# Attention, a wide MLP and a top-1 expert layer on one core: where the last rows are written, what GpSimd computes, and where the smallest expert runs

## The chip, the cores and the metric

The kernel runs on one core of a Trainium2 chip. The metric is the device time of one execution in microseconds (us). The kernel before took 583.51 us (median of three runs, 580.92 to 584.21); lower is better.

## The reference

```python
def _attn_ref(q, k, v, w1, b1, w2):                  # 2 x 8 heads, 576 positions, head size 64
    scores = (1.0 / np.sqrt(D)) * np.matmul(q, k.transpose(0, 1, 3, 2))
    x = (np.log1p(np.abs(rel)) / np.log1p(np.maximum(pos[:, None], 1.0)))[..., None]
    scores = scores + (np.maximum(x @ w1 + b1, 0.0) @ w2).transpose(2, 0, 1)[None]
    attn = softmax(scores)                           # over the keys
    return np.matmul(attn, v)

def _moe_ref(x, w_in, w_out):                        # 1152 x 512 -> 2048 -> 512
    h = x @ w_in
    sp = np.where(h > 20.0, h, np.log1p(np.exp(np.minimum(h, 20.0))))
    return (h * np.tanh(sp)) @ w_out

def _moe2_ref(x, w_gate, w1, w2, capacity):          # 8 experts, 512 -> 1024 -> 512, capacity 288
    expert_idx = np.argmax(x @ w_gate, axis=1)       # one expert per row
    # the first 288 rows of each expert are kept, the others give zero
    h = np.maximum(np.einsum('ecd,edf->ecf', disp, w1), 0.0)
    y = np.einsum('ecf,efd->ecd', h, w2)
    out[i] = gate_w[i] * y[expert_idx[i], pos[i]]    # gate_w: softmax probability of the expert

reference: x = attention heads joined to 1152 rows of 512; _moe_ref; _moe2_ref
```

## The kernel before

**Tiles.** Attention and the MLP go over five tiles of rows (`it` 0 to 4): four of 256 rows (128 of each batch) and one of 128, which holds the last 64 rows of both batches. Products that need precision are made of two half-precision terms: a "high half" (the value rounded to f16) and a "low half" (the rest), and three f16 matmuls high x high, high x low, low x high.

**Order.** Everything up to the first expert's inputs is a list of operations, each with one or more ways to run it (an engine, a cost in ns that the planner of the table believes, and the code). The table `ORDER` at the top holds, for every operation, its place and its way: `c // 8` is the operation, `c % 8` the way. `Plan.emit` issues them in that order, so each engine's queue is what the table says. Behind it (from line 1351) the experts are written in plain program order.

**MLP chain.** For each of 8 pairs of feature blocks (`mlp_a`, line 825) the chain from the first product's PSUM is: exp (ScalarE, 839), two steps on VectorE (840, 841), ln and exp (842, 843), a product (844, GpSimd or VectorE), a scaled product (845, VectorE), the high half (848) and the low half (849, GpSimd or VectorE), and then the second product (`mlp_b`). `split16` (316) makes the halves of the attention's output, `keys_split` (593) those of the keys, `slots` (1085) adds up which row goes to which place of the first expert (1100); all three have ways on GpSimd.

**Handover to the first expert.** `y_out` writes each tile's result rows to `yscr` in DRAM (951; for the last tile 981 and 982). The first expert is the one that row 0 chose. `first_rows` computes from the first four tiles which rows it gets (`gid0`, line 1136) and gathers them in three indirect DMAs from GpSimd (1139). `first_slots` then places them: for each of four blocks of 128 features it multiplies the three gathered chunks (f32, 96 rows each) with a masked unit matrix `dg` and the last tile's rows, still in SBUF (`yx`), with a 0/1 matrix `m_`, both in f32, into one PSUM bank; a high and a low half of that bank go to `xT`. `first_loads` has meanwhile loaded the expert's weights and made the halves of the first one (1246 to 1262).

**Experts.** `experts_list` (1327) sorts the chosen experts, the first first and the smallest last; its numbers go to registers. `expert(k)` loads the next first weight (`load1`), runs `gemm1(k)` (8 blocks of 12 matmuls; in it the halves of this expert's second weight, `halves(k, 1, i)`, and behind block 0 the last piece of the expert before, `finish(k - 1)`), reads the next token table, gathers the next rows (`gather`), loads the next second weight (`load2`) and runs `gemm2(k)` (4 groups of 24 matmuls; in it the next expert's halves, its transposed rows `xt`, and `back`, which transposes results to rows). `sized` computes a weight's scale from four sums of squares (`square`). `scatter` writes the rows to the output, three indirect DMAs. Token tables and lists (`tb`, `gid`, `tid`) have two buffers. If the last expert has at most 48 rows, `few` (1477) runs it: with the rows as the stationary operand, in f16 halves like the others. In these inputs four experts are chosen; three run in full and the fourth has few rows.

Of the kernel before, what the change touches and what calls it, by code (L numbers as in the profile page):

```python
# [9 lines left out]
F32 = mybir.dt.float32  # L10
# [12 lines left out]
P = 128  # L23
# [266 lines left out]
def tile_kernel(ctx: ExitStack, tc: tile.TileContext, a: dict, cap: int):  # L290
# [794 lines left out]
    def slots(t):  # L1085
# [3 lines left out]
        def f():  # L1089
            ts(dve, si.t[:, 1:2], si.t[:, 0:1].bitcast(U32), e0s, ALU.subtract)  # L1090
            if t == 8:
                ts(dve, m_.t[:, 0:SL], sl16, si.t[:, 1:2], ALU.is_equal)
                return
# [48 lines left out]
    def first_slots(m_):  # L1142
# [13 lines left out]
        for ct in range(4):  # L1156
# [8 lines left out]
            def f(ps=ps, cc=cc):  # L1165
                pe.matmul(ps.t[:, 0:SL], y_.t[:, cc], m_.t[:, 0:SL], start=False, stop=True)
# [452 lines left out]
```

## Time and profile before

| | |
|---|---|
| median of three runs | 583.51 us |
| profiled execution | 582.39 us |
| its span, first to last instruction | 580.6 us |
| TensorE busy (matmuls; weight loads) | 500.1 us; 339.8 us |
| VectorE, ScalarE, GpSimd busy | 457.9, 392.8, 114.3 us |
| TensorE clock granted, mean | 0.943 of 2.4 GHz |
| DMA | 74.27 MB, mean 128 GB/s |

PE is TensorE's matmuls, PEld its weight loads, DVE is VectorE, ACT ScalarE, POOL GpSimd, SP SyncE (which issues DMAs). An engine with a q behind it (POOLq, SPq) is its queue. A row of a timeline is one instruction, or several alike in a row (x24): start, length, engine, line, operation, output<-inputs, shapes, and in brackets how long the engine stood idle before and what ended that.

### The profile page before, as it was taken

To read this page: it belongs to the slowest core of one execution; us is meant where nothing else is said; L and a number is where in the kernel's file an instruction comes from. 1 tells how busy PE (TensorE), PEld (TensorE's weight loads), DVE (VectorE), ACT (ScalarE), POOL (GpSimd) and SP (SyncE) were. 2 spreads that over 40 slices of the span, in tenths; PEclk is the share of its full clock that TensorE was granted. 3 is DMA by queue.
4 is the path that set the end of the run, shared out by engine and by line. 5 is a ranking of instruction groups with operands and counts; after the bars stand their busy time and mean duration, and the time that the engine had idled before them with its cause. 6 is when DMAs were issued, how large, how long until landed. Compare 5 with 4: busy or idle time off the path is not lost. (4 is left out here: it accounts for less than half of the span.)

```text
span 580.6 us, 12111 instructions
## 1 busy us (share of the span) xinstructions
PE 500.1 (86%) x4521; PEld 339.8 (59%) x4521; DVE 457.9 (79%) x1163; ACT 392.8 (68%) x791; POOL 114.3 (20%) x143
## 2 busy tenths in 40 slices
PE   5565888989999988999999899999983598999775
PEld 4111556765666653555687557896472477777532
DVE  8999999998884898999869845699788275867363
ACT  5889999988575768999956714656741057877361
POOL 2000000011122326200011602125341201112120
PEclk9975699989999999999999999999997599999879
DMA  8987973700110123546244022050010147666210
GB/s 330 362 330 243 330 277 112 278 22 1 59 37 1 65 103 102 172 160 208 78 124 120 0 76 61 34 201 1 1 39 10 51 161 244 192 193 204 88 33 16
DMA packets 28347, 74.27 MB, mean 128 GB/s; under 512 B 4870, under 2 KB 4998, under 8 KB 26224
## 3 DMA queue, kind: packets, MB, share of 16 engines
q1 hardware_dynamic: 26576, 69.21, 34.8%
q0 software_dynamic: 1696, 4.11, 2.3%
q8 instruction: 40, 0.66, 0.5%
q14 instruction: 35, 0.29, 0.2%
HBM read 55.67 MB, written 17.87 MB: 127 GB/s over the span
## 5 line engine op out<-in xcount | busy, mean ns | idle before, releaser
L834 PEld LDWEIGHTS <-WIt 128*128 128x128 f16 x960 | 85.3, 98 | 15.2 <-issue 5.6
L867 PE MATMUL pb<-WOt,ra 128*128 128x512 f16 x336 | 78.0, 379 | 1.6 <-DVE ra L849 0.7
L834 PE MATMUL pb<-PX,WIt 128*128 128x256 f16 (+1 forms) x696 | 74.8, 265 | 3.0 <-DVE rr L306 1.7
L654 ACT ACTIVATE ra<-ra,rm 128x576 f32<-128x576 f32 x62 | 47.9, 774 | 17.8 <-DVE rm L653 17.8
L867 PEld LDWEIGHTS <-ra 128*128 128x128 f16 x336 | 31.9, 98 | 39.7 <-issue 3.7
L309 DVE SCALAR_TENSOR_TENSOR W<-AT,wsc,W 128x1024 f16<-128x1024 f32 x32 | 40.6, 1280 | 15.2 <-ACT W L1402 14.8
L517 PE MATMUL pb<-ra,w2s 128*32 128x512 f32 (+17 forms) x268 | 35.8, 541 | 16.0 <-ACT ra L506 6.9
L506 ACT ACTIVATE ra<-AT,stab 128x528 f32<-128x528 f32 (+16 forms) x67 | 41.2, 650 | 4.6 <-DVE PX L309 2.1
L653 DVE CUSTOM_DVE_ANT_0 ra<-ps,ra 128x576 f32<-128x576 f32 x50 | 36.5, 752 | 9.2 <-PE ps L636 8.2
L726 PE MATMUL pb<-ra,AT 128*64 128x128 f32 (+1 forms) x700 | 40.7, 267 | 0.7 <-ACT ra L665 0.7
L844 POOL TENSOR_TENSOR ra<-ra,ra 128x512 f32<-128x512 f32 (+1 forms) x13 | 15.5, 1195 | 129.1 <-DVE gl L323 90.3
L1446 PE MATMUL py<-HH,W 128*128 128x288 f16 x288 | 39.3, 294 | 0.9 <-ACT HH L1420 0.7
L726 PEld LDWEIGHTS pb<-ra,AT 128*64 128x64 f32 x700 | 35.2, 139 | 5.5 <-issue 1.8
L662 PE MATMUL pb<-ident,ra 128*128 128x128 f32 x201 | 31.8, 290 | 3.8 <-ACT ra L665 1.9
L1446 PEld LDWEIGHTS <-W 128*128 128x128 f16 x288 | 29.0, 101 | 8.9 <-issue 1.3
L1417 PEld LDWEIGHTS <-W 128*128 128x128 f16 x288 | 28.2, 98 | 9.5 <-DVE W L309 1.4
L1197 ACT ACTIVATE jk<-AT 128x1024 bf16<-128x1024 f32 x28 | 29.5, 1055 | 2.1 <-DMA AT<-m 1.9
L662 PEld LDWEIGHTS pb<-ident,ra 128*128 128x128 f32 x201 | 23.5, 147 | 11.4 <-ACT ra L654 4.8
L309 DVE SCALAR_TENSOR_TENSOR rw<-rw 128x1024 int32<-128x1024 int32 x24 | 29.2, 1222 | 0.3
L531 ACT ACTIVATE rbe<-pb,rl 128x511 f32<-128x511 f32 (+41 forms) x53 | 24.8, 489 | 6.0 <-PE pb L517 2.9
L834 PE MATMUL ps<-PX,WIt 128*128 128x256 f16 (+1 forms) x264 | 27.6, 258 | 0.0
L842 ACT ACTIVATE ra<-ra,two 128x512 f32<-128x512 f32 (+1 forms) x21 | 13.6, 646 | 17.9 <-DVE ra L309 14.8
(444 smaller groups left out, 1149.8 us busy)
## 6 DMA issues: line engine op xcount, KB each, us to landing
AT<-m SPq DMA_DIRECT2D x32, 512.0 KB, 4.7
bscr<-rbe SPq DMA_DIRECT2D x36, 295.5 KB, 2.2
rw<-wo SPq DMA_DIRECT2D x8, 1024.0 KB, 4.6
ra<-bscr SPq DMA_DIRECT2D x27, 288.0 KB, 3.4
rw<-wi SPq DMA_DIRECT2D x4, 1024.0 KB, 12.0
WOt<-wi SPq DMA_DIRECT2D x4, 1024.0 KB
AT<-k SPq DMA_DIRECT2D x4, 576.0 KB, 7.1
out<-rw SPq DMA_DIRECT2D x9, 256.0 KB, 3.2
```

What stands on the lines that cost most here:

```text
L309: (eng or dve).scalar_tensor_tensor(out=out, in0=in0, scalar=s, in1=in1, op0=op0, op1=op1)
L506: on_act = lambda h_=h_, g=g: act.activation(h_.t[:, 0:dn], T[:, 0:dn], AF.Relu, bias=stab[:, g:g + 1])
L517: pe.matmul(ps.t[32 * c:32 * c + 32, 0:d1 - d0], w2s, hs[c].t[:, d0:d1], start=True, stop=True)
L653: op("DVE", c_dve(S), lambda i=i, own=own, m_=m_, b_=b_: dve.tensor_tensor_reduce(out=own(), in0=blk(s_.t[:, 960 * i:960 * i + S]), in1=bl ...
L654: op("ACT", c_act(S, 2), lambda i=i, m_=m_, col=col: act.activation(t_.t[:, S * i:S * i + S], t_.t[:, S * i:S * i + S], AF.Exp, bias=m_.t[ ...
L662: pe.transpose(pa.t[:, P * j:P * j + P], t_.t[:, 384 * n + P * j:384 * n + P * j + P], ident)
L726: pe.matmul(ov[64 * i:64 * i + 64, ct % 2, w * bb:w * bb + w], v_, t_.t[:, at + c0:at + c0 + w], start=n == 0, stop=n == 4)
L834: pe.matmul(ps.t[:, n * f_:n * f_ + n], WI[:, wv, ct, P * ft:P * ft + P], xt.t[:, xv, ct, 0:n], start=i == 0, stop=i == 11)
L867: pe.matmul(y_.t, gv()[:, g2, c:c + P], WO[:, wv, ft], **kw)
L1197: act.activation(j.rearrange("p (a b) -> p a b", a=2) if m else j, raw(m, i), AF.Square, accum_out=sca(k, m, i))
L1417: pe.matmul(ps[:, 0:SL], W1[:, wv, ct, P * ft:P * ft + P], XT[k % 2][:, xv, ct], start=i == 0, stop=i == 11)
L1446: pe.matmul(ps[:, 0:SL], W2[:, wv, ft, P * dt:P * dt + P], HH[:, hv, ft], start=ft == 0 and i == 0, stop=ft == 7 and i == 2)
```

## The change

- The last tile's two writes to `yscr` wait until the three gathers of the first expert are through (`r=[y_] + [("g0", c) ...]`).
- The gathered rows and the last tile's rows are split into f16 halves first; `first_slots` places high and low halves with separate f16 matmuls (two groups per feature block), and their PSUM banks are copied to `xT` each by itself.
- The ways on GpSimd go from `split16`, `keys_split`, `mlp_a` (844, 849) and `slots` (1100). Some believed costs change. There is a new `ORDER` table.
- In the experts: token tables and lists have three buffers; for k above 0, `sized` moves from block 1 to block 2 of `gemm1` and the halves one block on; the second weight's third high half goes from ScalarE to VectorE; expert 1's four squares move from `gemm1(0)` to the start of `gemm2(0)`, its sizing one group on.
- `few` goes. The expert with few rows runs inside its neighbour (`with_few`): its weights are loaded to buffers of their own before the neighbour's first product, its rows are gathered behind that product, and its f32 matmuls stand between the groups of the neighbour's second product.

The table, decoded by operation, changes these engines: line 844 from 25 on GpSimd and 15 on VectorE to 40 on VectorE; line 849 from 28 and 12 to 40; line 1100 from 2 and 4 to 6; `split16` in `x_out` from 11 on GpSimd, 12 on VectorE, 1 on ScalarE to 15 on VectorE, 9 on ScalarE; line 602 from 8 on GpSimd to 3 on VectorE, 5 on ScalarE; line 531 from 21 on VectorE to 10, line 665 from 34 to 26, line 710 from 9 to 4, the others of these to ScalarE; line 1261 from 2 on VectorE to none. On VectorE, behind the last tile's routing, the new table has, in this order: one low half of the first weight, the row list, the last rows' high half, the low half of gather 0, `dg`, the halves of gathers 1 and 2, the last rows' low half, `m_`, the sizing of the second weight, the last low half of the first weight, three copies to `xT`.

```diff
-        op("POOL", c_pool(m, 2.1), lambda: pool.tensor_tensor(out=nv(), in0=nv(), in1=uv(), op=ALU.mult), r=[u_], w=[n_], alt=[("DVE", ...)])
+        op("DVE", c_dve(m), lambda: dve.tensor_tensor(out=nv(), in0=nv(), in1=uv(), op=ALU.mult), r=[u_], w=[n_], lk=1)
...
-            dma(lambda: yscr[512:576], lambda: yv()[:64], 131072, r=[y_], p=["yscr"])
+            h_ = pl.buf(R2)
+            hv = lambda v: h_.t.bitcast(F16)[:, DM * v:DM * v + DM]
+            op("ACT", c_act(DM, 1, 50), lambda: act.activation(hv(0), ps.t, AF.Identity, scale=col(1)), r=[ps, y_], w=[h_], alt=[("DVE", ...)])
+            op("DVE", c_dve(DM, 1.04, 1), lambda: stt(hv(1), ps.t, col(1), hv(0), ALU.mult, ALU.subtract), r=[ps, y_], w=[h_])
+            dma(lambda: yscr[512:576], lambda: yv()[:64], 131072, r=[y_] + [("g0", c) for c in range(NCH)], p=["yscr"])
...
+            for v in range(2):
+                ps = pl.buf(RB)
+                def f(ps=ps, cc=cc, v=v):
+                    for c in range(NCH):
+                        pe.matmul(ps.t[:, CS * c:CS * c + CS], xg0[c][1](v)[:, cc], dg.t.bitcast(F16)[:CS, CS * c:CS * c + CS], start=c == 0, stop=False)
...
+                    pe.matmul(ps.t[:, 0:SL], yv(v)[:, cc], m_.t.bitcast(F16)[:, 0:SL], start=False, stop=True)
...
-    tb = [es(f"tb{i}", [CS, NCH, 2], I32) for i in range(2)]
+    tb = [es(f"tb{i}", [CS, NCH, 2], I32) for i in range(3)]
...
-            if k and ft == 1:
+            if k and ft == 2:
                 sized(k, 1, PO[0])
...
-            if ft > 1 and ft < 6:
-                halves(k, 1, ft - 2)
-            if more and ft > 3:
+            if ft > 1 + bool(k) and ft < 6 + bool(k):
+                halves(k, 1, ft - 2 - bool(k))
+            if k and more and ft > 3:
                 square(k + 1, 0, ft - 4, W["j"])
...
+    def few_rows():
...
+        dve.tensor_copy(tidf, sel[:, 0, 0:1])
+        ts(dve, gidf, sel[:, 0, 0:1], float(NT - 1), ALU.min)
+        pool.indirect_dma_start(out=xgf, out_offset=None, in_=yscr, in_offset=bass.IndirectOffsetOnAxis(ap=gidf[:, 0:1], axis=0))
+    def few_x():
+        for ct in range(4):
+            pe.transpose(PT[0][:, CS * ct:CS * ct + CS], xgf[:, P * ct:P * ct + P], ident[:CS, :CS])
+        act.copy(XF.rearrange("p c n -> p (c n)"), PT[0][:, 0:4 * CS])
+    def few_h(i):
+        for ct in range(4):
+            pe.matmul(PH[i][:CS], XF[:, ct], R1f[:, ct, 512 * i:512 * i + 512], start=ct == 0, stop=ct == 3)
...
+    def few_y(i):
+        for ft in range(4 * i, 4 * i + 4):
+            pe.matmul(PH[0][:CS], HF[:, ft], R2f[:, ft], start=ft == 0, stop=ft == 7)
+    def with_few(k):
+        few_loads()
+        if k:
+            gemm1(k, False)
+        few_rows()
+        def between(dt):
+            if dt == 0:
+                few_x()
+            if dt < 2:
+                few_h(dt)
+            if dt:
+                (few_flip if dt < 3 else few_y)((dt - 1) % 2)
+        gemm2(k, False, between)
+        finish(k)
+        few_y(1)
+        act.activation(OC[:, 0], PH[0][:CS], AF.Copy, scale=sel[:, 0, 1:2])
+        pool.indirect_dma_start(out=a["out"], out_offset=bass.IndirectOffsetOnAxis(ap=tidf[:, 0:1], axis=0), in_=OC[:, 0], in_offset=None, ...)
...
-        with tc.If(nv > k + 1) as more:
+        with tc.If(nf > k + 1) as more:
...
-            if k:
-                last(k)
-            else:
-                gemm2_last(k)
+            with tc.If(nv > k + 1) as more_:
+                with_few(k)
+            with more_.Else():
+                last(k)
```

## Rows read from the trace of the kernel before

**Rows 1.** Stage windows: busy us of each engine (x instructions), granted clock, DMA share, GB/s.
```profile
200.00:280.00 80.00, 75.22 (x659) 41.14 (x658) 74.62 (x210) 68.31 (x152) 20.66 (x18) 1.00 0.44 148
280.00:440.00 160.00, 153.50 (x1668) 114.35 (x1667) 122.16 (x354) 91.15 (x195) 48.05 (x51) 1.00 0.21 63
...
444.50:455.40 10.90, 0.03 (x1) 0.00 (x0) 6.96 (x16) 0.00 (x0) 4.99 (x4) 0.50 0.23 67
455.40:464.80 9.40, 8.40 (x32) 7.21 (x33) 2.19 (x7) 1.12 (x3) 0.00 (x0) 0.61 0.08 16
...
559.00:574.20 15.20, 14.67 (x56) 7.51 (x56) 8.80 (x19) 5.21 (x9) 2.67 (x2) 0.80 0.14 38
```

**Rows 2.** Timelines of VectorE, SyncE, GpSimd and TensorE at the handover.
```profile
440.26 0.17 DVE L306 TENSOR_SCALAR gid<-smsk 96x3 uint32<-96x3 f32 x1
...
445.35 10.59 SPq L330 DMA_DIRECT2D yscr<-rw  x2
...
449.85 2.13 POOL L1139 DMA_INDIRECT ra<-yscr,gid  x1 [0.30 <-issue]
452.28 0.91 POOL L1139 DMA_INDIRECT ra<-yscr,gid  x1 [0.30 <-issue]
...
455.47 1.14 PE L1162 MATMUL pb<-rw,ra 96*128 96x96 f32 x4 [10.95 <-DMA ra<-yscr,gid]
...
464.86 3.10 PE L1417 MATMUL ph<-xT,W 128*128 128x288 f16 x24 [0.99 <-DVE xT L1169]
```

**Rows 3.** Timelines of TensorE, GpSimd and VectorE, third expert's second product.
```profile
533.92 3.10 PE L1446 MATMUL py<-HH,W 128*128 128x288 f16 x24
...
541.18 4.78 PE L1446 MATMUL py<-HH,W 128*128 128x288 f16 x24
...
536.60 0.94 POOL L1385 DMA_INDIRECT xg<-yscr,gid  x1 [0.79 <-issue]
...
540.58 0.17 DVE L1388 CAST tid<-tb 96x3 uint32<-96x3 int32 x1 [4.76 <-DMA out<-OC,tid]
```

**Rows 4.** Timeline of GpSimd: the last scatters.
```profile
560.90 1.74 POOL L1431 DMA_INDIRECT out<-OC,tid  x1 [2.07 <-DMA out<-OC,tid]
564.77 0.92 POOL L1431 DMA_INDIRECT out<-OC,tid  x1 [2.13 <-DMA out<-OC,tid]
575.11 0.92 POOL L1518 DMA_INDIRECT out<-OC,tid  x1 [9.42 <-ACT OC L1517]
```

**Rows 5.** Groups of instructions, whole span: xcount | busy us, mean ns | idle before.
```profile
L849 POOL TENSOR_TENSOR ra<-ra,ra 128x512 f16<-128x512 f32 x14 | 17.1, 1221 | 33.7 <-ACT ra L848 15.2 <-DVE ra L848 9.8 <-PE pb L968 5.4
...
L844 DVE TENSOR_TENSOR ra<-ra,ra 128x512 f32<-128x512 f32 x3 | 2.0, 675 | 0.0
...
L306 DVE TENSOR_SCALAR ra<-ra 128x512 f32<-128x512 f32 x14 | 8.4, 604 | 8.5 <-ACT ra L839 8.5
L306 DVE TENSOR_SCALAR ra<-rw 128x512 f32<-128x512 f32 x9 | 3.8, 423 | 5.4 <-ACT rw L839 5.4
...
L1166 PE MATMUL pb<-rw,rw 128*128 128x288 f32 x8 | 4.1, 634 | 0.0
...
L1169 DVE TENSOR_TENSOR xT<-pb,xT 128x288 f16<-128x288 f32 x4 | 1.7, 455 | 1.0 <-ACT xT L1168 1.0
```

**Rows 6.** Timeline of VectorE: end of the handover list, and of the third expert's first product.
```profile
446.39 0.75 DVE L306 TENSOR_SCALAR W<-AT,wsc 128x1024 f16<-128x1024 f32 x1
...
451.62 0.15 DVE L1325 COPY cnt<-pb 1x8 f32<-1x8 f32 x1
...
533.72 1.28 DVE L309 SCALAR_TENSOR_TENSOR W<-AT,wsc,W 128x1024 f16<-128x1024 f32 x1
534.92 0.82 DVE L309 SCALAR_TENSOR_TENSOR HH<-pt,HH 128x288 f16<-128x288 f32 x2
```

**Rows 7.** Timelines of TensorE (second product of the first expert) and VectorE (a sizing).
```profile
480.11 0.28 PE L1446 MATMUL py<-HH,W 128*128 128x288 f16 x1 [0.73 <-ACT HH L1420]
...
525.63 0.91 DVE L306 TENSOR_SCALAR wsc<-wsc 128x1 int32<-128x1 int32 x5
```

More of the change, by code (lines that the diff above doesn't have):

```diff
@@ L1099, in slots @@
         if t > 1:
[L1100 removed]
+            op("DVE", c_dve(SL, 0.52), lambda: dve.tensor_tensor(out=acc[b], in0=acc[b], in1=m_.t.bitcast(F16)[:, 0:SL], op=ALU.add), r=[m_], w=[("acc", b)], lk=1)
     xg0 = []
@@ L1347, in experts_list @@
         tsum(fl[:, 0:E], v64)
+        ts(dve, A, ef[0:1], 1.0, ALU.add, fl[:, E:E + 1], ALU.is_equal)
+        dve.tensor_tensor(out=A, in0=A, in1=fl[:, 0:E], op=ALU.mult)
+        tsum(fl[:, E + 2:E + 3], A)
+        ts(dve, fl[:, E + 1:E + 2], fl[:, E + 1:E + 2], float(HC + 1), ALU.is_lt)
+        dve.tensor_tensor(out=fl[:, E + 1:E + 2], in0=fl[:, E:E + 1], in1=fl[:, E + 1:E + 2], op=ALU.subtract)
         dve.tensor_copy(lst[:, 1:], fl[:, 1:])
@@ L1387, in tokens @@
     def tokens(k):
[L1388 removed]
+        dve.tensor_copy(tid[k % 3], tb[k % 3][:, :, 0])
     def summed(k, m):
@@ L1436, in back, with gemm2 @@
             pe.transpose(po[:, c], YT[:, dt, CS * c:CS * c + CS], ident)
-        dve.tensor_tensor(out=OC[:, :, P * dt:P * dt + P], in0=po, in1=tb[k % 2][:, :, 1:2].bitcast(F32).to_broadcast([CS, NCH, P]), op=ALU.mult)
-    def gemm2(k):
-        summed(k + 1, 0)
+        dve.tensor_tensor(out=OC[:, :, P * dt:P * dt + P], in0=po, in1=tb[k % 3][:, :, 1:2].bitcast(F32).to_broadcast([CS, NCH, P]), op=ALU.mult)
+    def gemm2(k, more=True, between=None):
+        if more:
+            if k == 0:
+                for i in range(4):
+                    square(1, 0, i, W["j"])
+            summed(k + 1, 0)
         for dt in range(4):
@@ L1447, in gemm2 @@
             act.activation(YT[:, dt], ps[:, 0:SL], AF.Copy, scale=sca(k, 0, 7))
-            if dt == 0:
-                sized(k + 1, 0, PO[1])
-            if dt == 2:
-                for c in range(NCH):
-                    xt(k + 1, c, (PT + PH)[c % 4])
-            if dt == 1 or dt == 2:
-                halves(k + 1, 0, 2 * dt - 2)
-                halves(k + 1, 0, 2 * dt - 1)
-            if dt > 1:
+            if more:
+                if dt == (k == 0):
+                    sized(k + 1, 0, PO[1])
+                if dt == 2:
+                    for c in range(NCH):
+                        xt(k + 1, c, (PT + PH)[c % 4])
+                if dt == 1 or dt == 2:
+                    halves(k + 1, 0, 2 * dt - 2)
+                    halves(k + 1, 0, 2 * dt - 1)
+            if dt > 0:
+                back(k, dt - 1)
+            if more and dt > 1:
                 square(k + 1, 1, 2 * dt - 4, W["j"])
                 square(k + 1, 1, 2 * dt - 3, W["j"])
-            if dt > 0:
-                back(k, dt - 1)
+            if between:
+                between(dt)
     def finish(k):
@@ L1511, in few, with few_loads @@
+    def few_loads():
+        sp.dma_start(tbf, tv[bass.ds(evf[0], 1)].rearrange("o p c w -> (o p) c w"))
+        for ct in range(4):
+            sp.dma_start(R1f[:, ct], a["m1"][bass.ds(evf[0], 1), P * ct:P * ct + P].rearrange("o p f -> (o p) f"))
+        for i in range(4):
+            sp.dma_start(R2f[:, 2 * i:2 * i + 2], a["m2"][bass.ds(evf[0], 1), 2 * P * i:2 * P * i + 2 * P].rearrange("o (c p) n -> p (o c) n", p=P))
+    def few_rows():
         for c, m in ((0, 0), (NCH - 1, 1)):
-            ts(dve, sel[:, c, 0:1], t_[:, c, 0:1], hm[:, m:m + 1], ALU.mult)
@@ new lines, in few_h, with few_flip @@
+    def few_h(i):
+        for ct in range(4):
+            pe.matmul(PH[i][:CS], XF[:, ct], R1f[:, ct, 512 * i:512 * i + 512], start=ct == 0, stop=ct == 3)
+        if i:
+            ts(dve, hs[:, 512:1024], PH[1][:CS], 0.0, ALU.max)
+        else:
+            act.activation(hs[:, 0:512], PH[0][:CS], AF.Relu)
+    def few_flip(i):
+        for j in range(4):
+            pe.transpose(PT[i][:, CS * j:CS * j + CS], hs[:, 512 * i + P * j:512 * i + P * j + P], ident[:CS, :CS])
+        dst, src = HF[:, 4 * i:4 * i + 4].rearrange("p f n -> p (f n)"), PT[i][:, 0:4 * CS]
+        if i:
+            dve.tensor_copy(dst, src)
+        else:
+            act.copy(dst, src)
@@ L1520, in last @@
     def last(k):
-        with tc.If(nl < HC + 1) as small:
-            few(k)
-        with small.Else():
+        if k:
             gemm1(k, False)
-            gemm2_last(k)
+        gemm2_last(k)
     def expert(k):
```

114 lines of the change are left out of this document (40 added, 74 removed), and 217 rows, old and new, of the table ORDER.

## The prediction

> **What bounds the kernel now.** I read the stage windows first, then the timelines of single engines where a stage has idle TensorE time, then the grouped instructions for prices. In the windows the reader sees three regimes [rows 1]. From 280 to 440 us TensorE is busy 153.5 of 160 us while VectorE has 122.2: the attention and MLP tiles are bound by TensorE, with little left to win. At the handover to the experts, 444.5 to 464.8 us, TensorE does 8.4 us of work in 20 us and its clock is granted at 0.50 to 0.61 (1.2 GHz for most of it). In the last expert, 559 to 574.2 us, the clock is 0.80 with TensorE nearly always busy.
>
> The timelines name the causes. At the handover the row numbers of the first expert (gid) are ready at 440.4 us, but the first of the two writes of the last rows, issued at 445.35 us, stands ahead of the gathers; the last two start at 449.85 and 452.28 us, and TensorE waits 10.95 us for them, until 455.47. The first expert starts at 464.86 [rows 2]. In the expert part TensorE has a hole at 537 to 540.8 us: VectorE's copy of the next token list waits 4.76 us for the scatter still reading its buffer; after the hole 24 matmuls take 4.78 us instead of 3.10 [rows 3]. At the end, scatters to the output go one after another, each waiting some 2.1 us for the one before [rows 4].
>
> The sum is made against the profiled execution, 582.39 us, with 580.6 of span and 1.8 around it; it lies 1.1 us under the median of 583.51 and inside the three runs.
>
> **GpSimd's arithmetic goes to VectorE (attention and MLP).** The issue table puts 53 products and differences of the MLP, 25 of line 844 and 28 of line 849, on VectorE, beside two sums of line 1100 and a few copies. On GpSimd one 128x512 takes 1.22 us, on VectorE 0.68 where it is least disturbed [rows 5]: at most 53 x 0.68 = 36 us more for VectorE. Against that the table moves 24 PSUM copies (11 of line 531, 8 of 665, 5 of 710) from VectorE to ScalarE, at about 0.5 us each (0.46 for 288 elements [rows 5]), 12 us. VectorE also gets back time that it now loses beside GpSimd: one form, 128x512 f32 of line 306, takes 604 ns in one group and 423 in another [rows 5], 2.5 us over 14 instructions in this group alone, and others are stretched alike. So VectorE's load grows by 24 us at most and perhaps not at all, against 38 us of idle time in 280 to 440 us [rows 1]. TensorE sets the pace there, with 6.5 idle us in that stretch and 4.8 in 200 to 280. The two GpSimd steps of each MLP chain become shorter by half, so part of these gaps should close, while the new order may open others. Bounds: 9 faster (nearly all gaps close), 6 slower (half as many again open). I take -3, near the small end, because what is gained in latency is mostly hidden behind TensorE.
>
> **Handover.** The write now follows the gathers, so these start some 0.8 us after gid (GpSimd's delay in the next such gather [rows 3]), at 441.2, with one every 1.24 us; the last lands 3.2 us after its start, as now (452.28 to 455.47) [rows 2], at 446.9. This wait is gone; next late is VectorE. It finishes its present list of small steps at 451.77 [rows 6]. The new list leaves out one high half and one low half of the first weight (0.74, 1.28; the high half goes to ScalarE) and adds: the low half of the last rows and those of three gathers (4 x 0.68), one high half of a gather (0.42), the sizing of the second weight (1.4), three copies to xT (3 x 0.46) [rows 5 to 7]. That is 451.8 - 2.0 + 5.9 = 455.7, against 464.86: -9.2. The placement itself, 8.4 us on TensorE at a clock of 0.61 [rows 1], runs as sixteen groups of one-pass f16 matmuls instead of eight f32 ones; they lie beside VectorE's list, behind the last low half at about 451. What is lost: in the kernel before, the f32 placement had brought the clock to 1.00 before the first expert. With less work ahead of it part of the expert's matmuls may run at 1.2 GHz; the hole at 537 us shows the price, 4.78 - 3.10 = 1.7 us [rows 3]. I add 1.0. Handover -8.2; bounds -11 (TensorE's own chain is the limit) and -4 (VectorE's list a further 4 us late).
>
> One rule speaks against this part. By the row, one of three gathers took 2.13 us instead of 0.91 beside VectorE work, and that is all [rows 2]. By the Trainium skill (SBUF — State Buffer, section Who interferes with whom) GpSimd and VectorE take their common port pair for a whole instruction, and descriptors written by GpSimd wait for VectorE in its two-port modes. By that rule, if all three gathers took 2.13, the last would land 3.6 us later, at 450.5, 1 us after VectorE wants it: 577.3 in place of 576.3.
>
> **First expert's second product.** The sizing of the next weight moves one block of matmuls later and its four squares leave the first product. The hole there, 0.73 us before 480.11, goes [rows 7]; the halves of that weight then come up to 1.3 us later (VectorE's sizing steps behind a later block), and the next product needs the last of them at once. Net 0, bounds +-1.5.
>
> **Halves of the second weight, experts 1 and 2.** Sizing moves from block 1 to block 2 of the first product (a block of 12 matmuls is 1.47 us), and one more high half (0.74) goes to VectorE. Now the last low half starts at 533.72 and the last two halves of HH end at 535.74, 1.8 us behind the product's end at 533.92, without harm [rows 6]. 2.2 us later, they end 4.0 us behind it, and the second product's first group, 2.95 long, needs them: +1.4 per expert. For expert 1 that is +1.4 (0 to +1.5); expert 2 is in the tail. The few rows' 4 MB of weights now load beside expert 2's gathers: +0.5 (0 to 1.5) for a late gather.
>
> **The few-row expert inside expert 2.** Counted from the end of the first product, T0 = 533.92, the kernel now ends 46.7 us later. New, in order: the first group of 24 ends at 4.4 (above). VectorE's last half of HH ends at 4.0; six small steps for the row list at 0.17 [rows 3] take 1.0; 0.8 of GpSimd's delay, 0.9 of issue and 2.3 of landing [rows 2, 3] put the gathered few rows at 9.0. TensorE stands before their transposes from 4.4 to 9.0: the same kind of hole as now at 537 us, which itself goes because token lists have three buffers. Transposes and the copy (about 0.5 each, with the hand-over): 10.3. Four f32 matmuls of 512 columns: line 1166 takes 4.1 us for four of 288 columns at a clock of 0.61 [rows 5], so 0.9 us each at 2.4 GHz and 1.8 at 1.2. Half of these four at 1.2 GHz: 5.5, to 15.8. Then 24 matmuls 2.95, transposes 0.33, four f32 3.6, transposes 0.65: 23.3; 24 matmuls and two sets of transposes 3.9: 27.2; 24 matmuls, 0.33, four f32 3.6 and the last transposes 0.33: 34.4. The first scatter, 0.8 behind: 35.2. Each next one waits for the one before, 0.92 + 2.13 = 3.05 [rows 4]; the few rows' scatter is fourth in that queue and ready at about 39, so it goes at 44.4, and the kernel ends 5.5 us behind the last scatter's issue, as now (575.11 to 580.6): 49.9. Tail 49.9 - 46.7 = +3.2. Bounds: -6 (the hole is half as long at full clock, and the few rows' scatter needn't queue) to +6 (f32 at 1.2 GHz throughout).
>
> **Sum.** -3 -8.2 +0 +1.4 +0.5 +3.2 = -6.1; 582.39 - 6.1 = 576.3 us.
>
> **Rivals.**
> 1. The tail gains too. For it: what used to be 14.7 busy us after 559 us [rows 1] is now spread between matmuls, and the hole at 537 us is gone. It needs a few-row gather that lands before TensorE asks for it. Tail -6 instead of +3.2, the late halves harmless (-1.4): 565.7.
> 2. VectorE becomes the bound of the tiles (slower). Place: the stretches where it is already full, 200 to 280 us with 74.6 of 80 busy [rows 1]. Price: 36 us more work in four full tiles and a ninth part is 8 per tile; with some 2.7 idle us per 40 us there, 5 spill over in each of three tiles, +15 in place of -3. It decides once the time that VectorE gets back from GpSimd and ScalarE is under half of what it takes over. 576.3 + 18 = 594.3; half-way 585.3.
> 3. The handover gives little: VectorE's list is later still and the clock stays at 1.2 GHz through the first expert's first product (11.8 us of it, so +5.9 instead of +1.0), which leaves -3.3: 581.2.
>
> **Chances.** Forecast 0.50 (own range 570 to 580.5), rival 1 0.24, rival 3 0.16, rival 2 0.10. A measurement of this kernel can't tell 0.5% from no change: 580.6 to 586.4 us. Faster: 0.48 of the forecast, rival 1, and 0.04 of rival 3: 0.76. Same: 0.02 and 0.12: 0.14. Slower: 0.10. Range: below 566 I leave half of rival 1, 0.10 with its edges; above 585 rival 2, 0.09.
>
> **What would show it.** Gathers of the first expert starting at 441 to 442 us before the write of the last rows; the first product's start 8 to 10 us earlier counted from gid; TensorE idle before the few rows' transposes for 3 to 6 us with the clock down behind it; four scatters in a row at the end with waits of 2.1 us and the last product long done. Wrong would be: TensorE idle over 20 us in 80 to 440 us; no hole before the few rows; the few rows' product as the last thing before the last scatter.

## The result and the profile after

The changed kernel takes 556.6 us (median of four runs, 554.0 to 558.3), the kernel before 582.2 beside it: ratio 0.956, 95% interval 0.950 to 0.961. The forecast of 576.3 had the direction right and the size far too small; the time lies below its range. The profiled execution took 556.07 us with a span of 554.3, 26.3 less than before.

The difference by stages, from the start of one group of matmuls on TensorE to the next (us):

| stage | before | after | difference | forecast |
|---|---|---|---|---|
| start to the end of the last MLP | 437.5 | 414.6 | -22.9 | -3 |
| to the first expert's first product | 27.3 | 16.3 | -11.0 | -9.2 |
| to the second expert's first product | 27.9 | 28.8 | +0.9 | +1.0 |
| to the third expert's first product | 27.6 | 32.1 | +4.5 | +1.9 |
| that product | 13.6 | 14.0 | +0.4 | 0 |
| from there to the end of the span | 46.7 | 48.5 | +1.8 | +3.2 |

The same stages in the stage windows (columns as in [rows 1]; the last row of before is one stretch more). Before:

```profile
0.00:108.50 108.50, 76.46 (x693) 41.41 (x693) 101.05 (x224) 94.64 (x188) 4.79 (x37) 0.86 0.77 282
108.50:437.50 329.00, 314.38 (x3038) 215.97 (x3037) 270.56 (x732) 226.80 (x476) 84.71 (x83) 0.99 0.25 80
437.50:464.86 27.36, 11.55 (x77) 9.64 (x77) 14.64 (x52) 2.80 (x8) 5.58 (x5) 0.63 0.12 32
464.86:533.92 69.06, 65.94 (x536) 52.40 (x536) 49.93 (x113) 49.47 (x89) 10.45 (x11) 1.00 0.62 194
533.92:580.60 46.68, 31.72 (x182) 20.42 (x179) 21.76 (x47) 19.11 (x32) 8.78 (x8) 0.87 0.19 64
...
0.00:200.00 200.00, 163.41 (x1426) 102.80 (x1427) 176.73 (x400) 163.21 (x321) 21.39 (x51) 0.91 0.48 175
```

After:

```profile
0.00:103.60 103.60, 75.79 (x692) 43.53 (x693) 95.93 (x215) 96.35 (x193) 5.29 (x37) 0.87 0.81 291
103.60:414.60 311.00, 308.30 (x3039) 216.28 (x3037) 272.86 (x780) 235.81 (x506) 10.21 (x9) 1.00 0.26 86
414.60:430.90 16.30, 7.32 (x78) 5.24 (x77) 14.28 (x54) 7.36 (x15) 3.98 (x4) 0.60 0.21 54
430.90:505.79 74.89, 69.48 (x537) 54.21 (x538) 51.08 (x119) 45.16 (x81) 12.48 (x12) 0.95 0.61 202
505.79:554.20 48.41, 31.42 (x154) 17.63 (x151) 7.89 (x18) 4.65 (x9) 4.65 (x5) 0.86 0.06 17
```

Three things are to be seen. Up to the end of the last MLP (first two rows) TensorE's idle time falls from 46.7 to 30.5 us. VectorE takes over 53 operations and is still busy 368.8 us in these rows, against 371.6 before. And in the fourth row TensorE's clock is no longer 1.00.

The timelines of the handover after the change answer to [rows 2] (VectorE, GpSimd, SyncE, TensorE):

```profile
415.75 0.17 DVE L307 TENSOR_SCALAR gid<-smsk 96x3 uint32<-96x3 f32 x1
...
416.83 0.93 POOL L1144 DMA_INDIRECT rw<-yscr,gid  x1 [4.41 <-PE pb L1330]
...
419.29 0.91 POOL L1144 DMA_INDIRECT ra<-yscr,gid  x1 [0.30 <-issue]
...
422.48 1.11 SPq L331 DMA_DIRECT2D yscr<-rw  x2
...
424.98 0.34 PE L1173 MATMUL pb<-ra,rw 96*128 96x96 f16 x2 [5.33 <-DVE rw L1149]
...
430.90 1.38 PE L1434 MATMUL ph<-xT,W 128*128 128x288 f16 x5 [0.59 <-DVE xT L1179]
```

The gathers start 1.1 us after the row numbers, ahead of the write, and TensorE now waits for VectorE's low half of the gathered rows, no longer for a gather. The timelines of TensorE, ScalarE, VectorE and GpSimd in the expert part answer to [rows 3, 4]:

```profile
476.03 0.77 PE L1467 MATMUL py<-HH,W 128*128 128x288 f16 x4 [0.84 <-DVE W L310]
...
491.81 2.01 PE L1434 MATMUL ph<-xT,W 128*128 128x288 f16 x12 [3.93 <-ACT jk L1206]
...
494.92 0.41 ACT L1437 ACTIVATE HH<-ph 128x288 f16<-128x288 f32 x1 [4.09 <-PE po L1453]
...
510.69 0.94 POOL L1516 DMA_INDIRECT xgf<-yscr,gidf  x1 [7.02 <-DVE gidf L307]
...
513.94 0.90 PE L1520 MATMUL pt<-ident,xgf 96*128 96x96 f32 x4 [3.99 <-DMA xgf<-yscr,gidf]
515.41 6.05 PE L1525 MATMUL ph<-R1f,XF 128*96 128x512 f32 x8 [0.57 <-ACT XF L1521]
...
539.99 0.94 POOL L1448 DMA_INDIRECT out<-OC,tid  x1 [28.37 <-DVE OC L1454]
...
549.52 0.92 POOL L1561 DMA_INDIRECT out<-OC,tidf  x1 [2.58 <-DMA out<-OC,tid]
```

The forecast hole before the few rows is there (3.99 us), with slow f32 matmuls behind it. Not forecast is the hole of 3.93 us before the third expert's first product. ScalarE has one like it (4.09 us, and it goes on 1.1 us after the first 12 matmuls behind the hole are done); VectorE's, 5.20 us, ends with a wait for ScalarE.

### The profile page after: what moved, and what is told of

Read it like the earlier page. It is cut to its first block, busy times and chain, and to the rows that moved or that the text cites. A ratio compares the mean times of both kernels' runs of the same rounds, so it can differ in the third digit from the quotient of the medians.

```text
span 554.3 us, 11929 instructions
## 1 busy us (share of the span) xinstructions
PE 492.3 (89%) x4493; PEld 336.9 (61%) x4493; DVE 442.0 (80%) x1180; ACT 389.3 (70%) x803; POOL 36.6 (7%) x67
## 4 chain that ended last, share of the span: by engine, by line
PE 53%; DMA 16%; DVE 16%; issue 9%; ACT 4%; SPq 2%; POOL 0%; another core or an unknown queue 0%; POOLq 0%; ACTq 0%; DVEq 0%
PE pb L868 15%; PE pb L835 9%; DMA out<-OC,tid 8%; PE ps L835 5%; PE pb L727 5%; PE pb L518 4%; PE pb L663 3%; DVE rw L310 3%; DVE ra L654 3%; DMA bscr<-rbe 2%; PE ps L633 2%; PE ps L663 2%; PE pb L872 2%; ACT ra L507 1%; DVE ra L307 1%
## 5 line engine op out<-in xcount | busy, mean ns | idle before, releaser
L868 PE MATMUL pb<-WOt,ra 128*128 128x512 f16 x276 | 64.4, 379 | 0.1
L654 DVE CUSTOM_DVE_ANT_0 ra<-ps,ra 128x576 f32<-128x576 f32 x50 | 36.6, 752 | 9.5 <-PE ps L637 6.7
L507 ACT ACTIVATE ra<-AT,stab 128x320 f32<-128x320 f32 (+17 forms) x69 | 42.2, 645 | 1.5 <-DVE stab L307 1.4
L310 DVE SCALAR_TENSOR_TENSOR W<-AT,wsc,W 128x1024 f16<-128x1024 f32 x24 | 30.6, 1282 | 6.4 <-ACT W L1419 6.0
L727 PEld LDWEIGHTS pb<-ra,AT 128*64 128x64 f32 x640 | 32.1, 138 | 4.8 <-issue 2.3
L310 DVE SCALAR_TENSOR_TENSOR rw<-rw 128x1024 int32<-128x1024 int32 (+1 forms) x25 | 29.8, 1195 | 0.0
L1054 POOL DMA_INDIRECT tbl<-pk,rm x9 | 10.9, 1211 | 273.3 <-DVE pk L1016 86.6
L532 ACT ACTIVATE rbe<-pb,rl 128x512 f32<-128x512 f32 (+47 forms) x57 | 25.7, 478 | 3.6 <-DMA bscr<-rbe 1.8
L619 PE MATMUL ps<-AT,rq 64*128 64x512 f32 x64 | 20.0, 703 | 8.2 <-DMA rq<-q 5.3
L663 PE MATMUL pb<-ident,ra 128*128 128x128 f32 x165 | 25.4, 283 | 1.7 <-ACT ra L655 0.9
L1434 PE MATMUL ph<-xT,W 128*128 128x288 f16 x144 | 22.4, 317 | 4.5 <-ACT jk L1206 3.9
L868 PE MATMUL pb<-WOt,rw 128*128 128x512 f16 x108 | 25.6, 379 | 0.0
```

The costliest lines, as they stand in the source:

```text
L310: (eng or dve).scalar_tensor_tensor(out=out, in0=in0, scalar=s, in1=in1, op0=op0, op1=op1)
L507: on_act = lambda h_=h_, g=g: act.activation(h_.t[:, 0:dn], T[:, 0:dn], AF.Relu, bias=stab[:, g:g + 1])
L532: op("ACT", c_act(n, 1, 50), lambda ends=ends: act.activation(*ends(), AF.Copy, scale=rl[:, blk:blk + 1]), r=[ps, "stab"], p=[be], alt=[(" ...
L654: op("DVE", c_dve(S), lambda i=i, own=own, m_=m_, b_=b_: dve.tensor_tensor_reduce(out=own(), in0=blk(s_.t[:, 960 * i:960 * i + S]), in1=bl ...
L663: pe.transpose(pa.t[:, P * j:P * j + P], t_.t[:, 384 * n + P * j:384 * n + P * j + P], ident)
L727: pe.matmul(ov[64 * i:64 * i + 64, ct % 2, w * bb:w * bb + w], v_, t_.t[:, at + c0:at + c0 + w], start=n == 0, stop=n == 4)
```

## Experiments

Times are medians; "+10.0" and the like are against the 556.6 of the changed kernel unless the kernel before is named. Ratios are against the kernel before, run beside each.

**GpSimd's 53 MLP operations back, new order.** In the table these are 25 codes of line 845 and 28 of line 850.

```diff
-op("DVE", ..., r=[u_], w=[n_], lk=1)
+op("DVE", ..., r=[u_], w=[n_], lk=1, alt=[("POOL", c_pool(m, 2.1), lambda: pool.tensor_tensor(...))])
 # the same for line 850; ORDER: code + 1 for the 53
```

> The changed kernel with the 53 MLP products and differences (25 and 28 operations) back on GpSimd, each at its place in the new issue table; nothing else differs. The last tile's MLP ends 22.9 us earlier in the changed kernel than before; this asks which part of the change did that. Theory A, the engine: GpSimd's arithmetic lengthens each MLP chain and stretches VectorE's instructions beside it, so most of the 22.9 us comes back: 571 to 579 us, VectorE's 128x512 forms at 0.85 to 0.97 us again in part. Theory B, the new order did it: within 4 us of the changed kernel, 555 to 561 us.

566.63 us, ratio 0.974 (0.970 to 0.977): +10.0, of which 8.8 by the end of the last MLP (423.4 against 414.6). This lies between the theories: GpSimd's arithmetic is a large part, but not most, of the 22.9 us. The stage windows of this kernel:

```profile
0.00:102.90 102.90, 76.07 (x692) 43.18 (x693) 95.88 (x215) 96.33 (x193) 5.28 (x37) 0.87 0.81 293
102.90:423.40 320.50, 311.07 (x3039) 215.97 (x3037) 270.50 (x727) 236.07 (x507) 75.36 (x62) 1.00 0.25 84
```

In the second row VectorE has 53 operations fewer (727 instead of 780), at most 36 us by its 0.68 each [rows 5], and is busy only 2.4 us less: what GpSimd takes off VectorE it takes back by slowing it. Less work alone can't make the end later. What grows is VectorE's idle time, up to the end of the last MLP from 45.8 to 57.0 us, and 7.7 us of it are now waits for GpSimd's two steps of the chain (VectorE's waits: waiting instruction <- awaited one: us in total, times, longest us):

```profile
DVE ra L312 <- POOL ra L847: 5.8, 5, 2.6
DVE ra L309 <- POOL ra L852: 1.9, 1, 1.9
```

**The same 53 on VectorE, old order.**

```diff
 # kernel before; ORDER: code + 1 (VectorE's way) for the same 53 operations
```

> The kernel before, with the same 53 operations on VectorE at their old places in the old issue table; nothing else differs. Theory A, the engine: most of the 22.9 us comes without the new table, 560 to 568 us. Theory B, the order: no gain, since the old order counts on two engines side by side, 578 to 588 us. In between would say that the engine and the table each bring a part.

587.96 us, ratio 1.012 (1.006 to 1.017): 5.3 us slower than before. Theory A fails here: without a new order the move itself loses.

**GpSimd busy for nothing, new order.** The extra products run on a tile of their own, in halves of 256 columns.

```diff
+    def idle_pool(kind, it, fp, m):
+        if 100 * kind + 10 * it + fp in ONPOOL:
+            for i in range(m // 256):
+                pool.tensor_tensor(out=pj, in0=pj, in1=pj, op=(ALU.mult, ALU.subtract)[kind])
```

> The changed kernel, with extra GpSimd products whose result nobody reads (as many 128x256 f32 halves as the 53 operations had) put at the places of the 53; VectorE still does the real ones. It takes away the latency of a GpSimd step in the MLP chain and leaves what its arithmetic does to VectorE beside it. Theory A1, VectorE is stretched: some 28 us of VectorE time comes back and half or more of it shows, 563 to 575 us. Theory A2, the latency of the chain: within 2 us of the changed kernel, 555 to 559 us, with VectorE's forms as short as without.

572.41 us, ratio 0.982 (0.978 to 0.985): +15.8, theory A1, with 19.4 us of VectorE time come back instead of 28. No step of the MLP waits for GpSimd here. The grouped instructions of VectorE (xcount | busy, mean ns | idle before) in the changed kernel, and then with GpSimd busy beside, its own group last:

```profile
L310 DVE SCALAR_TENSOR_TENSOR rw<-ra,rw 128x512 f32<-128x512 f32 x6 | 4.0, 684 | 0.1
...
L845 DVE TENSOR_TENSOR rw<-rw,ra 128x512 f32<-128x512 f32 x6 | 4.1, 684 | 0.0
```

```profile
L312 DVE SCALAR_TENSOR_TENSOR rw<-ra,rw 128x512 f32<-128x512 f32 x6 | 5.3, 892 | 0.1
...
L853 DVE TENSOR_TENSOR rw<-rw,ra 128x512 f32<-128x512 f32 x6 | 4.8, 806 | 0.0
...
L832 POOL TENSOR_TENSOR pj<-pj 128x256 f32<-128x256 f32 x95 | 75.7, 797 | 7.0
```

The same six instructions take 892 and 806 ns instead of 684. By the stage windows VectorE is busy 388.2 us up to the end of the last MLP, 19.4 more than without, and that end comes 14.2 us later:

```profile
0.00:104.40 104.40, 76.20 (x692) 43.73 (x693) 96.85 (x213) 96.64 (x193) 10.50 (x42) 0.89 0.80 288
104.40:428.80 324.40, 312.76 (x3039) 216.50 (x3037) 291.36 (x780) 236.26 (x506) 80.37 (x100) 1.00 0.25 83
```

**Order and engines crossed.** 281 operations changed engine in the table, many in pairs that cancel out.

```diff
 # kernel before; ORDER: its sequence, every operation on the engine of the new table
```

> The kernel before: its order of issue stays, and each of the 281 operations that the new table puts on another engine is put there (the 53 of GpSimd among them). With the 53 alone the old order was 5.3 us slower (587.96). Theory B1, the sequence: the old one still costs what it costs, 581 to 590 us. Theory B2, which engine does what (PSUM copies from VectorE to ScalarE, nothing on GpSimd): most of the 22.9 us that the tiles gained, 562 to 570 us.

```diff
 # changed kernel; ORDER: its sequence, the 281 on the engine of the old table
```

> The other corner: the changed kernel with its order of issue, and all 281 operations back on the engine that the table of before gave them. With only the 53 of GpSimd back it was 566.63. Theory B1, the sequence: 563 to 572 us, as with the 53 alone. Theory B2, the engines: the gain of the tiles is gone, 576 to 584 us.

615.01 us, ratio 1.055 (1.050 to 1.061), and 602.59, ratio 1.035 (1.029 to 1.040). Both theories fail: each mixture is slower than both kernels. Each of the two sequences is good only with the engines for which it was made.

**The other 228 back, the 53 on VectorE.**

```diff
 # changed kernel; ORDER: 228 of the 281 on the engine of the old table, not the 53
```

> The changed kernel with its order and with the 53 MLP operations on VectorE, but the other 228 operations whose engine the new table changed back on the engine of before. With the 53 alone back it was 566.63, with all 281 back 602.59. If the two parts add up, this is 556.6 + (602.6 - 566.6) = 592.6 (589 to 597). If GpSimd's arithmetic is what the 228 were changed for, they hardly matter without it: 557 to 565.

595.16 us, ratio 1.023 (1.017 to 1.028): +38.6. With the +10.0 of the 53 that makes 48.6, and both together cost 46.0: the two parts nearly add up. The 228 were not changed for the sake of GpSimd alone.

**24 PSUM copies back to VectorE.**

```diff
 # changed kernel; ORDER: VectorE's way for 11 of line 532, 8 of 666, 5 of 711
```

> The changed kernel with 24 of its PSUM copies (11 of the score, 8 of the probability and 5 of the reciprocal steps, as many as the table moved on balance) back from ScalarE to VectorE, where the kernel before had them, at their places in the new order. Theory L, VectorE's load: it rises by some 11 us beside 369 of 414.6, and most of that shows: 564 to 570 us. Theory B1, the fit of order and engine: where such a copy stands in VectorE's queue, it waits for what ScalarE need not wait for, and the time is more than the load: 572 us or more. Rival: VectorE has 46 idle us in the tiles, the copies fit in: 556 to 560 us.

569.38 us, ratio 0.978 (0.973 to 0.983): +12.8, theory L. The stage windows:

```profile
0.00:108.30 108.30, 77.72 (x692) 43.82 (x693) 97.42 (x221) 95.07 (x187) 5.27 (x37) 0.86 0.77 278
108.30:425.20 316.90, 309.44 (x3039) 216.75 (x3037) 279.64 (x798) 229.66 (x488) 10.01 (x9) 1.00 0.26 85
```

VectorE is busy 8.3 us more up to the end of the last MLP (377.1), and that comes 10.6 us later (425.2). VectorE's 46 idle us took up none of it.

**The write alone, in the kernel before.**

```diff
-    dma yscr[1088:1152] <- last rows, gather, gather, gather, dma yscr[512:576]
+    gather, gather, gather, dma yscr[512:576], dma yscr[1088:1152]
```

> The kernel before with one thing moved: the first of the two writes of the last rows is issued behind the three gathers of the first expert's rows, as the second already was. Theory H, the write held the gathers: they start near 441 us after the last MLP's own end of 437.5 (not 445 to 452), and the first product 7 to 9 us earlier, 573 to 576 us. Rival: VectorE's list is what sets the handover in the old code, the first product moves by at most 2 us, 580 to 583 us.

577.30 us, ratio 0.989 (0.982 to 0.996): 5.3 us faster than before, a little short of theory H. From the last MLP to the first product it is 22.1 us instead of 27.3. The timelines of GpSimd and TensorE (this execution was 5.5 us late from its first 108 us on, ahead of anything that the edit touches):

```profile
446.91 0.93 POOL L1141 DMA_INDIRECT rw<-yscr,gid  x1 [3.25 <-PE pb L970]
...
455.90 1.17 PE L1164 MATMUL pb<-rw,ra 96*128 96x96 f32 x4 [5.51 <-DVE rw L1155]
```

TensorE now waits for VectorE (the matrix of line 1155 behind VectorE's list): the next late thing is the one that the forecast named.

**The write undone, in the changed kernel.**

```diff
-    gather, gather, gather, dma yscr[512:576], dma yscr[1088:1152]
+    dma yscr[1088:1152], gather, gather, gather, dma yscr[512:576]
```

> The changed kernel with one thing undone: the second of the two writes of the last rows is issued as soon as its rows are ready, ahead of the gathers, as in the kernel before. In the kernel before, moving that write alone gave 5.3 us (577.30), about half of the 11.0 us by which the handover became shorter. Theory H: here it costs more than that, because nothing else covers the gathers: the first product starts 6 to 9 us later, 562 to 566 us. Rival: the low halves and VectorE's list set the handover here too, 557 to 560 us.

560.49 us, ratio 0.964 (0.960 to 0.968): +3.9, in between. The first product starts 20.8 us behind the last MLP instead of 16.3. GpSimd's timeline:

```profile
420.81 0.93 POOL L1146 DMA_INDIRECT rw<-yscr,gid  x1 [10.83 <-DVE rm L1053]
```

The first gather starts 8.7 us after the end of the last MLP (412.2), against 2.2 in the changed kernel. The order of the write is worth 4 to 5 us in either kernel; the other 6 of the 11.0 are the rest of the handover (placement in f16, VectorE's shorter list), which was not tried by itself.

**The hole before the third expert.** The test is turned round for the third expert alone.

```diff
-        with tc.If(nf > k + 1) as more:   # go on; Else: few rows or last
+        if k == 2:
+            with tc.If(nf < k + 2) as done:   # few rows or last
+                stop()
+            with done.Else():
+                go_on()
```

> The changed kernel with the test at the third expert turned round, so that the path that this data takes (few rows beside it) falls through and the other one jumps; the instructions that run are the same. In the changed kernel TensorE stands still for 3.9 us, from 487.9 to 491.8 us, and ScalarE for 3.9 us up to 494.8, each ending with its own taken branch. Theory C, the taken jump costs that: 3 to 4.5 us less, 552 to 554 us, and no hole before the third expert's first product. Rival: the code of the few-row path is new to the engines wherever it lies, so the hole stays: 555.5 to 558 us.

557.95 us, ratio 0.958 (0.955 to 0.961): no gain, as the rival had it, and yet theory C holds for the hole. The hole of 3.93 us is gone, and TensorE's timeline shows another one earlier:

```profile
485.87 0.90 PE L1424 MATMUL pt<-ident,xg 96*128 96x96 f32 x4 [2.79 <-DMA xg<-yscr,gid]
```

SyncE no longer jumps either, so that the few rows' weights are issued from 476.2 us on instead of 481.6, into the gather of the third expert's rows (issued from 476.0 on). What the jump had kept apart now runs together. If that is what makes the rows late, they must come sooner:

```diff
+    table(1), table(2) and the few rows' list loaded ahead of gemm1(0)
+    tokens(0); few_rows()            # few rows gathered ahead of gemm2(0)
-    gemm1(k); table(k + 1); gather(k + 1); tokens(k + 1)
+    gather(k + 1); tokens(k + 1); gemm1(k); table(k + 2)   # k > 0
```

> The changed kernel with the third expert's test turned round (as in the run before), and the row lists and gathers earlier: all lists are loaded ahead of the first expert, the next expert's rows are gathered before the first product instead of behind it, and the few rows before the first expert's second product. Theory D: the gathers no longer share the DMA engines with the few rows' weights, so both holes of TensorE go (3.93 us before the third expert's first product, 3.99 before the few rows' transposes), and with the second the slow clock behind it (6.05 us for 8 matmuls that take 3.6 to 4 later): 8 to 10.5 us less, 546 to 549 us. Rival: the few rows' weights, loaded earlier, take the time from the second weights' load and the hole comes back elsewhere: 553 to 558 us.

550.30 us, ratio 0.944 (0.938 to 0.949): -6.3, less than theory D's 8 to 10.5. Both holes are gone, and TensorE has a new one of 2.83 us in the first expert, for rows gathered behind the few rows' own.

```diff
+                if k == 1:
+                    few_rows()        # no longer ahead of gemm2(0)
```

> The version of the run before (test turned round, lists and gathers early; 550.30), with the few rows' list and gather moved from ahead of the first expert's second product to ahead of the second expert's first one. In the run before, TensorE waited 2.83 + 1.02 us at 452.7 to 457.6 for the second expert's rows, whose gather stood behind the few rows' on GpSimd, and 1.81 us at 447.1 for a sizing step behind their eight steps on VectorE. Theory: these three holes go, 3.5 to 6 us less: 544 to 547 us. Rival: the second expert's rows are late by themselves (their list is loaded behind the first weights), so the hole stays: 549 to 551 us.

551.03 us, ratio 0.949 (0.943 to 0.954), not the 544 to 547 of the theory. The same with the jump put back:

```diff
-        if k == 2: ... (the test turned round)
```

> The same, with the test at the third expert as in the changed kernel, so that the path that is taken is a jump again. Theory C (a taken jump holds each engine some 4 us): TensorE's hole before the third expert's first product is back, 3 to 4 us more than the run with the test turned round: 547 to 551 us. Rival: with early gathers the jump hides behind work that is still queued: within 1 us.

557.05 us, ratio 0.957 (0.952 to 0.963): 6.0 us more than with the test turned round, beyond the 3 to 4 of theory C. TensorE's timeline with the jump, and then without:

```profile
494.41 0.49 PE L1453 MATMUL po<-ident,YT 128*96 128x128 f32 x3
499.07 2.21 PE L1434 MATMUL ph<-xT,W 128*128 128x288 f16 x12 [4.17 <-issue]
```

```profile
453.34 0.90 PE L1424 MATMUL pt<-ident,xg 96*128 96x96 f32 x4 [2.90 <-DMA xg<-yscr,gid]
...
492.08 0.49 PE L1453 MATMUL po<-ident,YT 128*96 128x128 f32 x3
492.41 1.94 PE L1434 MATMUL ph<-xT,W 128*128 128x288 f16 x12
...
509.46 0.50 PE L1519 MATMUL pt<-ident,xgf 96*128 96x96 f32 x4
510.59 3.67 PE L1524 MATMUL ph<-R1f,XF 128*96 128x512 f32 x8 [0.63 <-ACT XF L1520]
```

The only edit is the jump: with it TensorE stands 4.17 us and waits for nothing that the profile shows ("issue"), without it there is no such gap. The rest of the 6.0 is not that hole: the transposes of line 1453 show TensorE already 2.3 us late ahead of it (494.41 against 492.08), 1.9 of them from the second expert's second product, where it waits for late halves. The very first row without the jump is the hole that spoiled that run: its rival was right, the second expert's rows are late by themselves. VectorE, which works out their row numbers, waits for their list, loaded behind the second expert's first weight (VectorE's timeline of the same run):

```profile
445.16 0.17 DVE L307 TENSOR_SCALAR gid<-tb 96x3 uint32<-96x3 int32 x1 [1.93 <-DMA tb<-tbl]
```
In the last row of the run without the jump, with the few rows there in time, the eight f32 matmuls take 3.67 us instead of 6.05.

**Halves one block earlier, as in the kernel before.**

```diff
-            if k and ft == 2:          # sizing; halves at ft - 3, two high halves on VectorE
+            if k and ft == 1:          # halves at ft - 2, one high half on VectorE
```

> The same as the first of these, with the sizing of the second weight and its halves in the first product one block earlier and three of four high halves on ScalarE, as in the kernel before. In the changed kernel the second expert's second product waits 0.84 us for the last low half (forecast +1.4). Theory: this wait goes, 0.5 to 1 us less per later expert, at most 2 us in all. Rival: ScalarE, with one high half more, is late for the halves of HH instead: 0 to 1 us more.

548.70 us, ratio 0.944 (0.939 to 0.948): the lowest median, 2.3 us under the run with the test turned round, though the runs of the two overlap (and 1.6 under the 550.30, from which it can't be told). The third expert's second product no longer waits (0.79 us in the changed kernel); the second expert's still does, 1.31 us, now for a half of HH. Its interval lies wholly below that of the changed kernel (0.950 to 0.961). Last:

```diff
-    for i in range(4): load1(1, i); then the lists
+    the lists; then for i in range(4): load1(1, i); gather(1) at ft == 5 of gemm1(0)
```

> The fastest version so far (halves early, 548.70) with the row lists loaded ahead of the second expert's first weight and its gather issued in the middle of the first product. There TensorE waited 1.14 us at 454.4 for these rows (2.90 in the version without the early halves). Theory: this hole goes, 1 to 3 us less, 545.5 to 548 us. Rival: the lists ahead of the weights delay the sizing of the first weight by as much: 548 to 550 us.

549.84 us, ratio 0.943 (0.935 to 0.950), no further gain: the rival. TensorE's timeline has the wait for rows exchanged for one on the sizing of the weight that is now loaded behind the lists:

```profile
450.62 0.49 PE L1209 MATMUL po<-ident,wsc 128*128 128x128 f32 x2 [3.73 <-DVE wsc L327]
```

## Why the forecast was wrong, step by step

**The tiles (-3 forecast, -22.9 measured).** This step failed: "the attention and MLP tiles are bound by TensorE, with little left to win" and "what is gained in latency is mostly hidden behind TensorE". The term was sized from TensorE's 11 idle us between 200 and 440 us [rows 1], 9 of them at most and 3 as taken. Three things were wrong with that. The gain in latency was not hidden: from the start of the second tile's MLP on (177.8 us before, 167.2 after) TensorE's idle time falls from 10.1 to 1.4 us, about the bound of 9. The stretch ahead of it, where TensorE idles 36.6 us before, is in no term, and 7.4 of them close. And the sum held TensorE's busy time fixed, which falls by 6.7 us for the same matmuls, about half of it on either side. By time, 10.6 us of the 22.9 lie ahead of the second tile's MLP and 12.3 behind its start. Most of these fall between the starts of the second and the third tile's MLP (stage windows, before and then after), where TensorE does not idle at all any more:

```profile
177.80:290.60 112.80, 108.02 (x969) 64.35 (x968) 98.50 (x286) 93.20 (x208) 26.08 (x24) 1.00 0.34 114
```

```profile
167.20:270.60 103.40, 103.40 (x956) 64.20 (x955) 96.86 (x286) 95.62 (x216) 2.61 (x2) 1.00 0.40 135
```

No rival of the forecast has a larger gain in the tiles. That the -22.9 is no accident of one execution is seen from the others: seven more runs with the changed kernel's tiles end the last MLP at 412.2 to 414.0 us, and the other run with the table of before (the write alone) at 443.1.

VectorE's time does count in the new order: 24 copies given back to it, 8.3 us of work, cost 10.6; 19.4 us of stretched instructions cost 14.2. But load is not all of it, since with GpSimd's steps back VectorE is busy 2.4 us less and the end still comes 8.8 later, while VectorE waits for GpSimd. The forecast's reading that VectorE's load grows "perhaps not at all" was right (368.8 against 371.6); it then took the effect on the time from TensorE's gaps alone.

What the runs show of the size: GpSimd's arithmetic, put back into the new order, costs 8.8 of the 22.9 us. The other 14, by subtraction, belong to the new table's sequence with its 228 other changes of engine, which can't be had in halves: the crossed tables cost 32 us more than the kernel before in one case and 20 in the other. Of the 22.9 us, 16.2 are idle time of TensorE that closed; the other 6.7 are busy time of TensorE. Where the experiments take some of the gain back, its busy time rises with the idle time too, 3.0 of 8.8, 3.1 of 10.6 and 4.9 of 14.2 us, about a third as here, so the two seem to have one cause; why the same matmuls take longer stays open. Open too is what a table planned anew for one of the two parts alone would give.

**The handover (-9.2 forecast, -11.0 measured)** was right in its mechanism: gathers ahead of the write, VectorE's list as the next late thing. Counted from the row numbers, the first product came after 15.0 us, forecast at 15.3 (455.7 against 440.4). The 1.6 us that bring it to the bound of -11 lie ahead of that: the row numbers start 1.1 us after the last MLP instead of 2.7. The +1.0 for the clock was +1.95 on the first 24 matmuls (5.05 us instead of 3.10, at a granted clock of 0.60 instead of 1.00). That the first expert as a whole still came out at +0.9 is luck: its second product, forecast at net 0, is 1.0 shorter (15.1 us instead of 16.1). Nor is the +1.95 fixed: in the thirteen runs with the new placement the first product takes 11.8 us at a clock of 1.00 in five, as before the change, and 12.7 to 14.2 at 0.82 to 0.93 in the other eight. One of the five is the version with the few rows' gather moved:

```profile
428.78:440.55 11.77, 11.77 (x96) 9.41 (x97) 9.70 (x33) 4.95 (x9) 0.00 (x0) 1.00 0.27 88
```

An estimate from the measured durations (5.05 us at 0.60, 3.10 at 1.00) makes the whole product at 1.2 GHz 11.8 us longer, and not 5.9 as rival 3 has it.

In the forecast one rule spoke against this step. The three gathers took 0.93, 0.92 and 0.91 us beside VectorE's work, so the 2.13 us of the rule's case did not come. By the Trainium skill (SBUF — State Buffer, section Who interferes with whom) a VectorE instruction with two SBUF inputs contends with a GpSimd instruction that reads SBUF. The run with GpSimd busy for nothing agrees, 806 ns instead of 684. The forecast's rule was about the gathers; the weight of sharing lay in the arithmetic.

**Late halves.** The wait of the second expert's second product was forecast at +1.4 and is 0.84. The late gather of the third expert's rows (+0.5) did not come: TensorE does not wait for them.

**The hole before the third expert** has no term in the forecast: 3.93 us. Its edit is "few-row expert inside its neighbour". In the kernel before, the tests of the first three experts fall through, and the jump comes at the fourth, behind the third expert's second product; in the changed kernel it comes at the third, ahead of that expert's first product. The prediction asked of each moved step what its instructions cost, and not what the branch around them does. It is the main part of the +4.5 where +1.9 was forecast.

**The tail (+3.2 forecast, +1.8 measured)** went as said: a hole of 3.99 us (4.6), the f32 matmuls behind it 6.05 (5.5), four scatters in a row with waits of 2.1 us and more, the last one the few rows'. The price of 0.9 us for an f32 matmul at 2.4 GHz was met (3.60 us for the four of the second group), but by luck: 4.1 us for four of 288 columns at a clock of 0.61 gives 1.1, and 0.9 only if the clock is taken as 0.50.

## What to carry to other kernels

Read the windows of the whole span before naming the bound: the 200 us that were left out held 37 of the 47 us that TensorE idled up to the end of the last MLP, and nearly half of the tiles' gain came ahead of 178 us. Do not hold the busy time of the bounding engine fixed. Where two engines are both busy 85% and more, ask what a microsecond more on either costs the end, and expect work moved to GpSimd to come back in part as slower VectorE instructions and as waits for GpSimd. A written-out order and its choice of engines are one thing: part of either, applied alone to the kernel before, lost 1 to 6%. Where a path is chosen at run time, lay the likely one so that it falls through, and look at what the jump keeps apart: here the turned test alone gained nothing.

## What the runs showed of the hardware

The jump to the few rows' path held TensorE 4.17 us and ScalarE 4.36 us in the run with the jump put back, 3.93 and 4.09 in the changed kernel; a branch that falls through shows no gap. By the Trainium skill (Runtime: NRT & Kernel Launch, section Instruction fetch mechanics) a taken branch whose target isn't in the engine's present window of instructions stalls until the page is fetched. The runs agree that a taken branch stalls; what is fetched meanwhile they do not show. 4 us is no fixed price. In the changed kernel the DMA engines were full at that time with the few rows' weights. Where the kernel before takes its jump they were nearly idle, and ScalarE stood 1.77 us (the kernel before's stage window and ScalarE's timeline, then the changed kernel's window):

```profile
553.50:558.50 5.00, 1.30 (x8) 0.63 (x6) 3.52 (x7) 3.23 (x7) 0.63 (x1) 0.99 0.03 8
558.53 0.92 ACT L1483 COPY XS<-xT 128x384 f16<-128x384 f16 x2 [1.77 <-issue]
```

```profile
487.80:491.80 4.00, 0.09 (x1) 0.08 (x1) 2.41 (x4) 3.01 (x7) 0.00 (x0) 1.00 1.03 396
```

Whether the load (a DMA share of 1.03 against 0.03) or the length of the jump makes the difference was not tried. SyncE pays it as well, which delays whatever loads stand behind its jump; taking the jump away moved those loads 5.3 us forward (4.1 against the gather beside them), and the gather came late.

VectorE's 128x512 instructions with two operands in SBUF took 684 ns alone and 806 to 892 in the mean with GpSimd's arithmetic beside them, while GpSimd's gathers beside VectorE kept to 0.91 to 0.93 us in the changed kernel.
